# Two pieces ahead, a clamp on another engine, squares on ScalarE and transposes in one step, in a kernel of attention and a squared-ReLU feed-forward

## The chip, the cores and the metric

The kernel runs on one core of one Trainium2 chip. The metric is the device time of one execution in microseconds (us). Five engines work side by side, each on its own instructions in the order in which they were issued: PE (matmuls), DVE (vector operations), ACT (activation functions and copies), POOL (vector operations) and SP, which here issues all the large DMAs. An engine that needs another's result waits on a semaphore, and everything behind the waiting instruction on its engine waits too. PE writes to PSUM, which the kernel uses as eight banks of 128 x 512 fp32.

## The reference

```python
def _attn_ref(q, k, v, g_q, g_k):          # q, k, v: (8, 12, 448, 64)
    def rmsnorm(x, g):
        rms = np.sqrt(np.mean(x * x, axis=-1, keepdims=True) + 1e-06)
        return x / rms * g
    q_n, k_n = (rmsnorm(q, g_q), rmsnorm(k, g_k))
    scores = 1.0 / np.sqrt(64) * np.matmul(q_n, k_n.transpose(0, 1, 3, 2))
    scores = scores - np.max(scores, axis=-1, keepdims=True)
    attn = np.exp(scores)
    attn = attn / (np.sum(attn, axis=-1, keepdims=True) + 1e-09)
    return np.matmul(attn, v)
...
x = attn_out.transpose(0, 2, 1, 3).reshape(3584, 768)
h = np.maximum(x @ w_in, 0.0)              # w_in: (768, 2048)
return h * h @ w_out                       # w_out: (2048, 768)
```

The inputs are fp32, but the feed-forward weights come to the kernel as 8-byte floating point words and are converted on the chip.

## The kernel before

The heads are worked on in pairs: 8 batches of 6 pairs, 48 in all. A pair has four steps (`n` or `m` from 0 to 3, 112 keys each). In a step PE computes the scores of both heads (`weigh`, L212), ACT takes the exponentials out of two PSUM banks (L214), and PE multiplies the previous pair's weights with its values (`attend`, L272) and with ones for the sums (L279, or L283 where DVE and POOL have added the weights up first, `add_up`). A reciprocal of the sums (L294) and a product (`finish`, L304) on DVE give the pair's part of x.

Ahead of this a pair is prepared: `load_qk` three pairs ahead, `square` (ACT, L154) at step 1 and `normalize` at step 2 of the pair two before it (sums on DVE, L162 and L163; the power -1/2 on POOL, L167; q times it on POOL into a tile `qn`, L172; the factor of k goes into the exponential). `turn` (L191) transposes q and k on PE into a bank; DVE evicts q with the gain (L193), ACT evicts k (L195). In the first 12 pairs (`alone`) the transposes of q go to bank 2 and those of k to bank 3, at steps 0 and 2 of the pair before; scores use banks 0 and 1 in even steps and 2 and 3 in odd ones. Later pairs use bank 2 for both transposes.

The feed-forward takes two batches as a unit, and unit u runs beside the attention of unit u + 1, as a generator that is advanced in proportion to the steps; the last unit runs alone at the end. So the span has four stages: attention alone (first 12 pairs), then attention with units 0, 1 and 2 of the feed-forward, then unit 3. A unit has 4 blocks. A block is two rounds of first products and one round of second products, each in Strassen's manner with seven products (names P1 to P7) in place of eight. Costs are counted in units: 18 for a first product, 126 for a round, 502 for a block, 2008 for a unit. `hidden` finishes a part of the middle values: DVE adds (L422), ACT takes the Relu (L423), POOL squares (L424). The second products begin with the 64 left-over rows of each batch (L451) and go on with L468; DVE and ACT add up the results (L499, L501).

The weights are converted in 64 pieces of 128 x 384, four to a tile. `load_weights` brings 8-byte words into a tile `words`; `split_words` scales the high words on ACT (L568), clamps them on POOL (L569) and turns the low words into numbers on ACT (L573, L574); `join_words` builds fp32 on DVE (L583, L587, L591). After a tile's fourth piece, four sums of pieces are made, DVE and POOL in turn (`make_sums`, L617), and the tile is stored to DRAM for the later units (L619). One call of `convert` makes sums, joins the piece that is begun, loads the next and splits its own. Calls have due times: 16 pieces every 2.4 steps in stage 1 (`early`), and 48 beside unit 0 (`late`), at every 18 cost units in bursts, one at each block. The order of all of this on all engines is the order of the program, since the scheduling is by hand.

`program` is built twice, with and without a shift of the scores; the inputs take the one without.

Of the kernel before, what the change touches and what calls it, by code (L numbers as in the profile page):

```python
# [10 lines left out]
F32 = mybir.dt.float32  # L11
# [7 lines left out]
P = 128  # L19
# [55 lines left out]
def program(ctx, tc, q, k, v, g_row, moe_w_in, moe_w_out, out, shift):  # L75
# [50 lines left out]
    def load_qk(i):  # L126
        b, c = pairs[i]
        qk = io.tile([CP, 2, 2 * NJ, D], F32, name="qk", tag="qk")
        nc.sync.dma_start(
            qk[:, 0].rearrange("p (h j) d -> p h (j d)", j=NJ),  # L130
            q[b, 2 * c : 2 * c + 2].rearrange("h (p j) d -> p h (j d)", j=NJ),
        )
        for e in range(2):
            nc.sync.dma_start(
                qk[:, 1].rearrange("p (j h) d -> p j h d", h=2)[:, :, e],
                k[b, 2 * c + e].rearrange("(p j) d -> p j d", j=NJ),
            )
        loaded[i] = qk
# [18 lines left out]
    def normalize(i):  # L157

        qk = loaded.pop(i)
        ms = small.tile([CP, 4 * NJ], F32, name="ms", tag="ms", bufs=2)  # L160
        for x, squares in enumerate(squared.pop(i)):
            nc.vector.tensor_reduce(out=ms[:, ts(x, 2 * NJ)], in_=squares, axis=AX.X, op=ALU.add)  # L162
        nc.vector.tensor_scalar(  # L163
            out=ms, in0=ms, scalar1=1.0 / D, scalar2=1e-6, op0=ALU.mult, op1=ALU.add
        )
        rr = small.tile([CP, 2, 2 * NJ], F32, name="rr", tag="rr", bufs=4)
        nc.gpsimd.tensor_tensor(  # L167
            out=rr.rearrange("p x r -> p (x r)"), in0=ms,
            in1=minus_half.to_broadcast([CP, 4 * NJ]), op=ALU.pow,
        )  # L170
        qn = att.tile([CP, NJ, 2, D], F32, name="qn", tag="qn", bufs=1)
        nc.gpsimd.tensor_tensor(  # L172
            out=qn.rearrange("p j h d -> p h j d"),
            in0=qk[:, 0].rearrange("p (h j) d -> p h j d", j=NJ),
            in1=rr[:, 0].rearrange("p (h j) -> p h j", j=NJ)[:, :, :, None].to_broadcast([CP, 2, NJ, D]),
            op=ALU.mult,
        )
        kn = qk[:, 1]
        if shift:
            nc.gpsimd.tensor_tensor(  # L180
                out=kn, in0=kn, in1=rr[:, 1, :, None].to_broadcast([CP, 2 * NJ, D]), op=ALU.mult
            )
        normal[i] = qn, kn.rearrange("p (j h) d -> p j h d", h=2), rr[:, 1]

    def turn(i, x):

        rows = normal[i][x]
        tr = banks[2 + x if alone(i) else 2][:, 0:S]
        dst = att.tile([P, S], F32, name="qT" if x == 0 else "kT")
        for j in range(NJ):  # L190
            nc.tensor.transpose(tr[:, ts(j, CP)], rows[:, j].rearrange("p h d -> p (h d)"), ident[:CP, :CP])  # L191
        if x == 0:
            nc.vector.tensor_scalar(out=dst, in0=tr, scalar1=g, scalar2=None, op0=ALU.mult)  # L193
        else:
            nc.scalar.copy(dst, tr)  # L195
        turned[i, x] = dst
# [5 lines left out]
    def weigh(i, m):  # L202

        if shift:
            return weigh_shifted(i, m)
        new_weights(i, m)
        qT, kT = turned[i, 0], turned[i, 1]
        odd = (2, 3) if alone(i) else (4, 6) if between(i) else (0, 1)
        scs = [banks[odd[e] if m % 2 else e][:CP, 0:S] for e in range(2)]
        for e, sc in enumerate(scs):  # L210
            r = ds(e * D, D)
            nc.tensor.matmul(sc, lhsT=kT[r, ts(m, CP)], rhs=qT[r, :], start=True, stop=True)  # L212
        for e, sc in enumerate(scs):
            nc.scalar.activation(  # L214
                weights[i, e, m], sc, AF.Exp, scale=normal[i][2][:, 2 * m + e : 2 * m + e + 1]
            )
        add_up(i, m)
# [14 lines left out]
    def weigh_shifted(i, m):  # L232
# [5 lines left out]
        for e in range(2):  # L238
# [4 lines left out]
            nc.vector.tensor_reduce(out=nmax, in_=sc, axis=AX.X, op=ALU.max, negate=True)  # L243
            w = att.tile([CP, S], F32, name="w", tag="rden", bufs=1)
            nc.scalar.activation(w, sc, AF.Exp, bias=nmax)
# [17 lines left out]
    def attend(i, m):  # L263
# [22 lines left out]
        if m == (NJ - 1 if alone(i) else 1):  # L286
            rden = att.tile([P, S], F32, name="rden", tag="rden", bufs=1)
            if shift:
                nc.vector.tensor_scalar(
                    out=rden, in0=den, scalar1=1e-9, scalar2=None, op0=ALU.add  # L290
                )
                nc.vector.reciprocal(out=rden, in_=rden)
            else:
                nc.vector.reciprocal(out=rden, in_=den)  # L294
            dens[i] = rden
# [4 lines left out]
    def finish(i):  # L300

        b, c = pairs[i]
        xT = new_x()
        nc.vector.tensor_tensor(out=xT, in0=values_bank(i), in1=dens.pop(i), op=ALU.mult)  # L304
        xts[b, c] = xT
# [115 lines left out]
    def hidden(dst, ps, part, op):  # L421
        nc.vector.tensor_tensor(out=dst, in0=ps, in1=part, op=op)  # L422
        nc.scalar.activation(dst, dst, AF.Relu)  # L423
        nc.gpsimd.tensor_tensor(out=dst, in0=dst, in1=dst, op=ALU.mult)  # L424

# [106 lines left out]
    all_pieces = list(weight_pieces())  # L532
    words, targets, sums_to_make = {}, {}, deque()

# [7 lines left out]
    def load_weights(n):  # L542
        if n >= len(all_pieces) or moe_w_in.dtype == F32:
            return
        kind, t, form, rows = all_pieces[n]
        words[n] = ffn_p.tile([P, HALF, 2], U32, name="words", tag="words")
        rows = rows.bitcast(U32)
# [16 lines left out]
    def split_words(n):  # L564
        if n not in words:
            return
        low, high = words[n][:, :, 0], words[n][:, :, 1]
        nc.scalar.activation(high.bitcast(F32), high.bitcast(F32), AF.Copy, scale=REBIAS)  # L568
        nc.gpsimd.tensor_scalar(  # L569
            out=high.bitcast(F32), in0=high.bitcast(F32), scalar1=MOST, scalar2=-MOST,  # L570
            op0=ALU.min, op1=ALU.max,
        )
        nc.scalar.activation(low.bitcast(F32), low, AF.Copy, scale=2.0**-29, bias=2.0**23)  # L573
        nc.scalar.activation(low, low.bitcast(F32), AF.Copy, bias=-(2.0**23))  # L574

    def join_words(n):
        kind, t, form, rows = all_pieces[n]
        dst = target(n)
        if n in words:
            both = words.pop(n)  # L580
            low, high = both[:, :, 0], both[:, :, 1]
            bits = dst.bitcast(U32)
            nc.vector.tensor_scalar(  # L583
                out=bits, in0=high, scalar1=4, scalar2=1,
# [16 lines left out]
    def make_weight_forms(kind, dst, t):  # L601
# [8 lines left out]
        sums_to_make.extend(todo)  # L610
        sums_to_make.append(((in_forms if kind == "in" else out_forms)[t], dst))

    def make_sums():

        for engine in (nc.vector, nc.gpsimd) if sums_to_make else ():
            to, left, right, op = sums_to_make.popleft()
            engine.tensor_tensor(out=to, in0=left, in1=right, op=op)  # L617
        if sums_to_make and len(sums_to_make[0]) == 2:
            nc.sync.dma_start(*sums_to_make.popleft())  # L619
# [42 lines left out]
    with tc.manual_schedule(engines=ENGINES):  # L662
# [8 lines left out]
        for i, (b, c) in enumerate(pairs):  # L671
            u = b // 2
            for n in range(NJ):
# [71 lines left out]
```

## Time and profile before

| | |
|---|---|
| median of three runs | 1703.6 us (1702.66 to 1704.24) |
| the profiled execution's own time | 1708.85 us |
| its span, first to last instruction | 1707.0 us |
| mean granted PE clock in it | 0.966 |
| loads of q, one for a pair | 48 of 224 KB |
| loads of k, two for a pair | 96 of 112 KB |
| loads of weight words | 64 of 384 KB |

Times in the profile are of one execution. A row of its timeline has the start in us, the length, the engine, the line of the kernel, what is written and read, and the count; in brackets stands how long the engine was idle before and what ended that. A row of the waits has the engine and line, what was waited for, the sum in us, the number and the longest. Matmuls overlap in PE's pipeline, so the length of a row is not its pace; the distance between starts is.

### The profile page before, as it was taken

The numbers are of one execution on the slowest core, as the hardware profiler recorded it, in microseconds if no ns is written. First come the engines' busy times: TensorE is split into PE (matmuls) and PEld (weight loads), VectorE is DVE, ScalarE is ACT, GpSimd is POOL, SyncE is SP. The second block draws the span as 40 slices with busy tenths as digits, with TensorE's granted clock in tenths as the row PEclk, the third lists the DMA queues.
The fourth block names the chain that finished last, engine by engine and source line by source line (L and its number), as shares of the span: only waits on it lengthen the run. The fifth ranks groups of instructions, "written<-read, shape, count | busy, mean of one in ns | idle before, by whom it ended". The sixth has DMA issues, their size and how long they took to land.

```text
span 1707.0 us, 14931 instructions
## 1 busy us (share of the span) xinstructions
PE 1573.1 (92%) x5204; PEld 719.2 (42%) x5204; DVE 808.6 (47%) x1170; ACT 554.3 (32%) x1033; POOL 614.1 (36%) x490
## 2 busy tenths in 40 slices
PE   5888897978969989999998999999998999999997
PEld 2222243433434434444444444444444444555554
DVE  2654546476676556343534445343535444213323
ACT  4554443452441423333131223333132221220120
POOL 4333545253353453424323354424223332210211
PEclk9999998988989989999999999999999999999999
DMA  3443213253242334303131324203131313132112
GB/s 97 121 127 113 86 46 125 63 164 118 63 159 100 125 116 145 100 25 133 54 123 49 111 77 162 90 19 137 49 122 49 128 38 139 65 125 88 65 74 67
DMA packets 98777, 164.65 MB, mean 96 GB/s; under 512 B 49028, under 2 KB 82820, under 8 KB 90500
## 3 DMA queue, kind: packets, MB, share of 16 engines
q1 hardware_dynamic: 98688, 163.60, 28.8%
q8 instruction: 43, 0.70, 0.2%
q14 instruction: 42, 0.34, 0.1%
q10 hardware_dynamic: 4, 0.00, 0.0%
HBM read 128.98 MB, written 34.60 MB: 96 GB/s over the span
## 4 chain that ended last, share of the span: by engine, by line
PE 72%; DVE 7%; issue 6%; POOL 6%; DMA 5%; ACT 3%; SPq 0%; POOLq 0%; ACTq 0%; DVEq 0%
PE bank L468 24%; PE bank L402 23%; PE bank L212 9%; PE bank L272 8%; PE bank L451 3%; DMA words<-in_moe_w_in_dram 3%; DMA words<-in_moe_w_out_dram 3%; PE bank L191 2%; DVE rden L294 2%; POOL rr L167 2%; POOL hid L424 2%; PE bank L279 1%; PE bank L283 1%; ACT wT L214 1%; ACT words L568 1%
## 5 line engine op out<-in xcount | busy, mean ns | idle before, releaser
L402 PE MATMUL bank<-xT,in_sb 128*128 128x448 f32 x1344 | 526.8, 546 | 2.5 <-DVE xT L304 2.5
L214 ACT ACTIVATE wT<-bank,rr 112x448 f32<-112x448 f32 x384 | 222.7, 628 | 438.8 <-PE bank L212 434.9
L402 PEld LDWEIGHTS bank<-xT,in_sb 128*128 128x128 f32 x1344 | 251.3, 192 | 255.5 <-issue 241.1
L468 PE MATMUL bank<-out_sb,hid 128*128 128x384 f32 x768 | 274.7, 487 | 2.1 <-DVE acc L501 2.1
L212 PE MATMUL bank<-qT,kT 64*112 64x448 f32 x768 | 220.3, 613 | 60.4 <-ACT wT L214 38.7
L167 POOL TENSOR_TENSOR rr<-ms,minus_half 112x16 f32<-112x16 f32 x48 | 150.7, 3140 | 339.6 <-DVE ms L163 329.6
L424 POOL TENSOR_TENSOR hid<-hid 128x448 f32<-128x448 f32 x128 | 123.1, 972 | 406.3 <-ACT hid L423 406.3
L501 DVE TENSOR_TENSOR acc<-acc,bank 128x384 f32<-128x384 f32 x324 | 173.4, 550 | 198.8 <-PE bank L468 161.1
L294 DVE RECIPROCAL rden<-bank 128x448 f32<-128x448 f32 x48 | 141.9, 2957 | 154.0 <-PE bank L283 99.6
L468 PE MATMUL bank<-out_sb,sums 128*128 128x384 f32 x576 | 214.3, 495 | 0.0
L272 PE MATMUL bank<-wT,vt 112*64 112x448 f32 x768 | 195.9, 591 | 3.6 <-DVE xT L304 3.6
L468 PEld LDWEIGHTS bank<-out_sb,hid 128*128 128x128 f32 x768 | 144.6, 190 | 105.7 <-issue 4.9
L422 DVE TENSOR_TENSOR hid<-bank,part 128x448 f32<-128x448 f32 x128 | 76.2, 615 | 177.9 <-PE bank L402 177.3
L409 ACT COPY part<-bank 128x448 f32<-128x448 f32 x128 | 67.7, 531 | 263.1 <-PE bank L402 263.1
L468 PEld LDWEIGHTS bank<-out_sb,sums 128*128 128x128 f32 x576 | 106.8, 192 | 83.5 <-issue 15.6
L212 PEld LDWEIGHTS bank<-qT,kT 64*112 64x112 f32 x768 | 62.8, 179 | 176.9 <-issue 77.0
L451 PE MATMUL bank<-out_sb,hid 128*128 128x384 f32 x256 | 100.7, 537 | 34.9 <-POOL hid L424 34.9
L423 ACT ACTIVATE hid<-hid 128x448 f32<-128x448 f32 x128 | 72.0, 576 | 179.1 <-DVE hid L422 179.1
L230 DVE TENSOR_TENSOR sum<-sum,wT 112x448 f32<-112x448 f32 x72 | 65.1, 904 | 122.8 <-ACT wT L214 120.1
L230 POOL TENSOR_TENSOR sum<-sum,wT 112x448 f32<-112x448 f32 x72 | 85.1, 1182 | 55.4 <-ACT wT L214 52.3
L272 PEld LDWEIGHTS bank<-wT,vt 112*64 112x64 f32 x768 | 39.6, 139 | 139.2 <-issue 122.6
L569 POOL TENSOR_SCALAR words<-words 128x384 f32<-128x384 f32 x64 | 40.9, 640 | 156.7 <-ACT words L568 156.7
(55 smaller groups left out, 1070.7 us busy)
## 6 DMA issues: line engine op xcount, KB each, us to landing
out_sb<-out_forms SPq DMA_DIRECT2D x24, 1536.0 KB, 7.5
in_sb<-in_forms SPq DMA_DIRECT2D x24, 1344.0 KB, 5.7
words<-in_moe_w_in_dram SPq DMA_DIRECT2D x32, 384.0 KB, 3.3
words<-in_moe_w_out_dram SPq DMA_DIRECT2D x32, 384.0 KB, 3.4
out_forms<-out_sb SPq DMA_DIRECT2D x8, 1536.0 KB, 6.1
qk<-in_q_dram SPq DMA_DIRECT2D x48, 224.0 KB, 2.7
qk<-in_k_dram SPq DMA_DIRECT2D x96, 112.0 KB, 2.9
vt<-in_v_dram SPq DMA_DIRECT2D x48, 224.0 KB, 2.8
```

The costliest lines, as they stand in the source:

```text
L167: nc.gpsimd.tensor_tensor(out=rr.rearrange("p x r -> p (x r)"), in0=ms, in1=minus_half.to_broadcast([CP, 4 * NJ]), op=ALU.pow,)
L212: nc.tensor.matmul(sc, lhsT=kT[r, ts(m, CP)], rhs=qT[r, :], start=True, stop=True)
L214: nc.scalar.activation(weights[i, e, m], sc, AF.Exp, scale=normal[i][2][:, 2 * m + e : 2 * m + e + 1])
L230: engine.tensor_tensor(out=sums[i, e], in0=sums[i, e], in1=weights[i, e, m], op=ALU.add)
L272: nc.tensor.matmul(av[ds(e * D, D), :], lhsT=values[i][:, e, m, :], rhs=weights[i, e, m], start=m == 0, stop=m == NJ - 1,)
L294: nc.vector.reciprocal(out=rden, in_=den)
L402: nc.tensor.matmul(ps, lhsT=w_sb[:, IN.index(left), c, :], rhs=forms[u, c][right], start=first and c == 0, stop=c == NK - 1, skip_group_ch ...
L422: nc.vector.tensor_tensor(out=dst, in0=ps, in1=part, op=op)
L424: nc.gpsimd.tensor_tensor(out=dst, in0=dst, in1=dst, op=ALU.mult)
L451: nc.tensor.matmul(ps, lhsT=flat[a][:, t, ds(FULL, P)], rhs=w_sb[t][:, 2 * a + half, :], start=a == 1 and t == 0, stop=a == 0 and t == 1,)
L468: nc.tensor.matmul(ps, lhsT=lefts[left][:, t, ts(tt, P)], rhs=w_sb[t][:, OUT.index(right), :], start=first and t == 0, stop=t == 1, skip_g ...
L501: nc.vector.tensor_tensor(out=acc, in0=acc, in1=ps, op=ALU.add)
```

## The change

- `load_qk` loads q as it loads k: one transfer for a head, the two heads side by side in rows. `normalize` multiplies q in place; the tile `qn` is gone.
- `turn` runs for x = 0 and 1 both at step 1 where the current pair is among the first 12, with banks 2 and 3; otherwise at steps 0 and 2 as before.
- The reciprocal is written into a buffer of the pool of x, and `finish` multiplies in place; the tile `rden` is gone.
- `hidden` squares on ACT.
- `words` has three buffers; pieces are loaded two ahead (a second load stands before the loop).
- The clamp moves from `split_words` on POOL to `join_words` on DVE.
- Stores of finished tiles have a queue of their own and are issued at the start of the first `convert` that finds no sums left; each list of conversions has one more slot at its end.

```diff
     def load_qk(i):
...
-        nc.sync.dma_start(
-            qk[:, 0].rearrange("p (h j) d -> p h (j d)", j=NJ),
-            q[b, 2 * c : 2 * c + 2].rearrange("h (p j) d -> p h (j d)", j=NJ),
-        )
-        for e in range(2):
-            nc.sync.dma_start(
-                qk[:, 1].rearrange("p (j h) d -> p j h d", h=2)[:, :, e],
-                k[b, 2 * c + e].rearrange("(p j) d -> p j d", j=NJ),
-            )
+        for x, rows in enumerate((q, k)):
+            for e in range(2):
+                nc.sync.dma_start(
+                    qk[:, x].rearrange("p (j h) d -> p j h d", h=2)[:, :, e],
+                    rows[b, 2 * c + e].rearrange("(p j) d -> p j d", j=NJ),
+                )
...
-        qn = att.tile([CP, NJ, 2, D], F32, name="qn", tag="qn", bufs=1)
-        nc.gpsimd.tensor_tensor(
-            out=qn.rearrange("p j h d -> p h j d"),
...
+        for x in range(2 if shift else 1):
             nc.gpsimd.tensor_tensor(
...
+                out=qk[:, x], in0=qk[:, x], in1=rr[:, x, :, None].to_broadcast([CP, 2 * NJ, D]),
+                op=ALU.mult,
             )
...
-        tr = banks[2 + x if alone(i) else 2][:, 0:S]
+        tr = banks[2 + x if alone(max(i - 1, 0)) else 2][:, 0:S]
...
-            rden = att.tile([P, S], F32, name="rden", tag="rden", bufs=1)
+            rden = new_x()
...
-        xT = new_x()
-        nc.vector.tensor_tensor(out=xT, in0=values_bank(i), in1=dens.pop(i), op=ALU.mult)
+        xT = dens.pop(i)
+        nc.vector.tensor_tensor(out=xT, in0=values_bank(i), in1=xT, op=ALU.mult)
...
         nc.scalar.activation(dst, dst, AF.Relu)
-        nc.gpsimd.tensor_tensor(out=dst, in0=dst, in1=dst, op=ALU.mult)
+        nc.scalar.activation(dst, dst, AF.Square)
...
-        words[n] = ffn_p.tile([P, HALF, 2], U32, name="words", tag="words")
+        words[n] = ffn_p.tile([P, HALF, 2], U32, name="words", tag="words", bufs=3)
...
         nc.scalar.activation(high.bitcast(F32), high.bitcast(F32), AF.Copy, scale=REBIAS)
-        nc.gpsimd.tensor_scalar(
-            out=high.bitcast(F32), in0=high.bitcast(F32), scalar1=MOST, scalar2=-MOST,
-            op0=ALU.min, op1=ALU.max,
-        )
...
             bits = dst.bitcast(U32)
+            nc.vector.tensor_scalar(
+                out=high.bitcast(F32), in0=high.bitcast(F32), scalar1=MOST, scalar2=-MOST,
+                op0=ALU.min, op1=ALU.max,
+            )
...
-        sums_to_make.append(((in_forms if kind == "in" else out_forms)[t], dst))
+        forms_to_store.append(((in_forms if kind == "in" else out_forms)[t], dst))
...
-        if sums_to_make and len(sums_to_make[0]) == 2:
-            nc.sync.dma_start(*sums_to_make.popleft())
...
     def convert(more):
+        for store in (forms_to_store.popleft(),) if len(sums_to_make) == 0 and forms_to_store else ():
+            nc.sync.dma_start(*store)
         make_sums()
...
-            load_weights(n + 1)
+            load_weights(n + 2)
...
-        return [(first + every * n, n < 4 * tiles) for n in range(4 * tiles + 3)]
+        return [(first + every * n, n < 4 * tiles) for n in range(4 * tiles + 4)]
...
     load_qk(1)
+    load_weights(1)
...
-                if n % 2 == 0 and i < last:
-                    turn(i + 1, n // 2)
+                if i < last:
+                    for x in range(2):
+                        if n == (1 if alone(i) else 2 * x):
+                            turn(i + 1, x)
```

More of the change, by code (lines that the diff above doesn't have):

```diff
@@ L170, in normalize @@
         )
-        qn = att.tile([CP, NJ, 2, D], F32, name="qn", tag="qn", bufs=1)
-        nc.gpsimd.tensor_tensor(
-            out=qn.rearrange("p j h d -> p h j d"),
-            in0=qk[:, 0].rearrange("p (h j) d -> p h j d", j=NJ),
-            in1=rr[:, 0].rearrange("p (h j) -> p h j", j=NJ)[:, :, :, None].to_broadcast([CP, 2, NJ, D]),
-            op=ALU.mult,
-        )
-        kn = qk[:, 1]
-        if shift:
+        for x in range(2 if shift else 1):
             nc.gpsimd.tensor_tensor(
-                out=kn, in0=kn, in1=rr[:, 1, :, None].to_broadcast([CP, 2 * NJ, D]), op=ALU.mult
+                out=qk[:, x], in0=qk[:, x], in1=rr[:, x, :, None].to_broadcast([CP, 2 * NJ, D]),
+                op=ALU.mult,
             )
-        normal[i] = qn, kn.rearrange("p (j h) d -> p j h d", h=2), rr[:, 1]
+        normal[i] = [qk[:, x].rearrange("p (j h) d -> p j h d", h=2) for x in range(2)], rr[:, 1]
     def turn(i, x):
-        rows = normal[i][x]
-        tr = banks[2 + x if alone(i) else 2][:, 0:S]
+        rows = normal[i][0][x]
+        tr = banks[2 + x if alone(max(i - 1, 0)) else 2][:, 0:S]
         dst = att.tile([P, S], F32, name="qT" if x == 0 else "kT")
@@ L214, in weigh @@
             nc.scalar.activation(
-                weights[i, e, m], sc, AF.Exp, scale=normal[i][2][:, 2 * m + e : 2 * m + e + 1]
+                weights[i, e, m], sc, AF.Exp, scale=normal[i][1][:, 2 * m + e : 2 * m + e + 1]
             )
@@ L243, in weigh_shifted @@
             nc.vector.tensor_reduce(out=nmax, in_=sc, axis=AX.X, op=ALU.max, negate=True)
-            w = att.tile([CP, S], F32, name="w", tag="rden", bufs=1)
+            w = ffn_p.tile([CP, S], F32, name="w", tag="part", bufs=4)
             nc.scalar.activation(w, sc, AF.Exp, bias=nmax)
@@ L532, in program @@
     all_pieces = list(weight_pieces())
-    words, targets, sums_to_make = {}, {}, deque()
+    words, targets, sums_to_make, forms_to_store = {}, {}, deque(), deque()
     def target(n):
@@ L568, in split_words @@
         nc.scalar.activation(high.bitcast(F32), high.bitcast(F32), AF.Copy, scale=REBIAS)
-        nc.gpsimd.tensor_scalar(
-            out=high.bitcast(F32), in0=high.bitcast(F32), scalar1=MOST, scalar2=-MOST,
-            op0=ALU.min, op1=ALU.max,
-        )
         nc.scalar.activation(low.bitcast(F32), low, AF.Copy, scale=2.0**-29, bias=2.0**23)
```

## The prediction

> **What bounds the kernel now.** I read the page first, then what TensorE (PE) waited for, then equal pieces of work in two stretches of the span, and last the order of time around single stalls.
>
> ```profile
> span 1707.0 us, 14931 instructions
> ...
> PE 1573.1 (92%) x5204; PEld 719.2 (42%) x5204; DVE 808.6 (47%) x1170; ACT 554.3 (32%) x1033; POOL 614.1 (36%) x490
> ...
> PEclk9999998988989989999999999999999999999999
> ...
> PE 72%; DVE 7%; issue 6%; POOL 6%; DMA 5%; ACT 3%; SPq 0%; POOLq 0%; ACTq 0%; DVEq 0%
> ```
>
> PE is the bound, yet 28% of the chain that ended last is not PE, and the granted clock shows an 8 only between the 7th and the 15th of the 40 slices. So the reserve lies in the early stages. The two stretches below go from the same place of the first feed-forward unit to the same place of the second (start of the second products of block 0 to those of block 3):
>
> ```profile
> 262.00:623.00 361.00, 303.61 (x916) 137.63 (x916) 223.78 (x320) 144.10 (x282) 150.77 (x137) 0.90 0.35 116
> 724.00:1005.00 281.00, 275.40 (x918) 127.39 (x919) 121.57 (x168) 83.97 (x154) 95.18 (x70) 0.99 0.24 84
> ```
>
> Columns: stretch, length, busy time and count of PE, weight loads, DVE, ACT, POOL, then clock, DMA share, GB/s. PE runs the same instructions (916 and 918), but the first stretch takes 80 us more. What differs is that weight pieces are converted in it: 152 more DVE instructions, 102 us of DVE. The largest single wait of PE shows how this costs time:
>
> ```profile
> 594.60 0.52 POOL L569 TENSOR_SCALAR words<-words 128x384 f32<-128x384 f32 x1
> 594.65 0.33 SPq L619 DMA_DIRECT2D out_forms<-out_sb  x1
> 595.10 0.36 SPq L554 DMA_DIRECT2D words<-in_moe_w_out_dram  x1
> ...
> 602.10 0.54 ACT L568 ACTIVATE words<-words 128x384 f32<-128x384 f32 x1 [12.44 <-DMA words<-in_moe_w_out_dram]
> ...
> 604.21 2.36 PE L212 MATMUL bank<-qT,kT 64*112 64x448 f32 x4 [9.50 <-ACT wT L214]
> ```
>
> A piece's load is issued only when the piece before the last is joined, here behind a 1.5 MB store. ACT, which works in order, stands 12.44 us before that piece, the exponentials queue behind it, and PE stands 9.50 us before a bank that they should have emptied. Then its four score matmuls take 2.36 us in place of 1.01.
>
> Stage 1 (the first 12 pairs, attention alone) has another limit:
>
> ```profile
> 34.65 1.01 PE L212 MATMUL bank<-qT,kT 64*112 64x448 f32 x4 [0.85 <-DVE qT L193]
> ...
> 48.03 1.01 PE L212 MATMUL bank<-qT,kT 64*112 64x448 f32 x4 [1.18 <-DVE qT L193]
> ...
> 50.62 1.01 PE L212 MATMUL bank<-qT,kT 64*112 64x448 f32 x4
> ...
> 53.22 0.60 PE L191 MATMUL bank<-ident,qk 112*128 112x112 f32 x4
> 53.75 1.69 PE L212 MATMUL bank<-qT,kT 64*112 64x448 f32 x4
> ...
> 61.43 1.01 PE L212 MATMUL bank<-qT,kT 64*112 64x448 f32 x4 [1.21 <-DVE qT L193]
> ...
> 77.42 1.84 PE L212 MATMUL bank<-qT,kT 64*112 64x448 f32 x4 [3.79 <-DVE qT L193]
> ...
> 121.69 1.84 PE L212 MATMUL bank<-qT,kT 64*112 64x448 f32 x4 [2.46 <-DVE qT L193]
> ...
> 187.49 1.01 PE L212 MATMUL bank<-qT,kT 64*112 64x448 f32 x4 [2.40 <-DVE qT L193]
> ```
>
> Each pair stops PE at step 1: the scores need bank 2, which the q transposes of step 0 have just filled and DVE has not yet emptied. At step 3 the same holds for bank 3 (1.69 instead of 1.01). From 34.65 to 187.49 are ten pairs: 15.28 us each. PE alone needs per step 2.60 (50.62 to 53.22) and per transpose group 0.53, so 4 x 2.60 + 2 x 0.53 = 11.46 us.
>
> **The change part by part.**
>
> *Both transposes at step 1 (stage 1).* They now fill banks 2 and 3 after the scores of step 1, and the next user is step 3, one whole step of 2.60 us later. DVE's queue decides whether that is enough:
>
> ```profile
> 62.47 1.16 ACT L214 ACTIVATE wT<-bank,rr 112x448 f32<-112x448 f32 x2 [1.72 <-PE bank L212]
> ...
> 70.55 2.96 DVE L294 RECIPROCAL rden<-bank 128x448 f32<-128x448 f32 x1 [4.88 <-PE bank L279]
> ...
> 76.69 0.67 DVE L193 TENSOR_SCALAR qT<-bank,g 128x448 f32<-128x448 f32 x1
> ```
>
> The reciprocal comes at the end of step 3, conversions may follow it, then the eviction of q. In the bad pair the reciprocal began at 70.55 and q was out at 77.36, 6.81 us later; scores of step 3 would come 2.60 (step 0) + 2.60 + 1.06 + 2.60 = 8.86 us after it. So even the bad pair fits. A new wait is added: the transposes need the exponentials of step 1 out of banks 2 and 3. These end 62.47 + 1.16 - 61.43 = 2.20 us after the scores start, and PE arrives after 2.60: 0.40 us of cover. Behind waiting transposes stands all of PE, behind the waiting ACT copy of k the squares and the next exponentials. Gain per pair: between nothing and 15.28 - 11.46 = 3.82 us. I take 12.2 us per pair, as the slow-clock pairs should go with the gaps but DVE grows: 10 x 3.08 = **31 us**, bounds 0 and 38.
>
> A rule bears on this. The Trainium skill, "TensorE: Matmul & The Clock Gate", Part 1, says that PE falls to half rate after an idle window of about 3.4 us. By it only the 3.79 us gap above should bring slow matmuls; the row at 121.69 shows 1.84 us after a gap of 2.46. So the trace disagrees, and short gaps are worth removing too; by the rule I would expect fewer slow pairs to vanish and some 10 us less.
>
> *Two pieces ahead, three buffers, stores one conversion later.* The load has a whole conversion more: at the pace of the second stretch (281 us for 1506 cost units) an 18-unit conversion is 3.36 us. In the stall above the data came 7.0 us after its issue, which two such intervals nearly cover. The ACT wait, and with it the score waits, should mostly go:
>
> ```profile
> PE bank L212 <- ACT wT L214: 38.7, 10, 9.5
> ```
>
> *Clamp from POOL to DVE, 64 times.* The trace has no such clamp on DVE. Nearest rows, of operations with the same size:
>
> ```profile
> L569 POOL TENSOR_SCALAR words<-words x64: 522/538/1253, 22.0 to 602.7; 128x384 f32<-128x384 f32 x64
> ...
> L583 DVE TENSOR_SCALAR in_sb<-words x32: 343/350/1975, 28.9 to 522.7; 128x384 uint32<-128x384 uint32 x32
> ...
> L587 DVE SCALAR_TENSOR_TENSOR in_sb<-words,in_sb x32: 557/559/2046, 29.3 to 523.1; 128x384 uint32<-128x384 uint32 x32
> ...
> L617 DVE TENSOR_TENSOR in_sb<-in_sb x16: 494/550/3895, 61.3 to 531.7; 128x384 f32<-128x384 f32 x16
> ```
>
> (minimum/median/maximum ns.) Bounds 0.34 and 1.98 us; I take 0.45, nearest L583, which reads the same words with the same kind of instruction. The hand-over ACT to POOL to DVE becomes ACT to DVE, so POOL's queue no longer delays a join. Is DVE full then? Conversions fill 990 of 1506 cost units of the stretch (108 + 342 + 342 + 198 by the lists of due times), 185 us at the second stretch's pace. In it DVE has 0.433 x 185 = 80 us of other work, 102 us of conversions as they ran, and about 43 clamps x 0.45 = 19: 201 us in 185. With all conversions at their short durations (0.35 clamp, 0.35, 0.56, 0.56 and half a sum 0.27, 2.1 us x 43 = 90) it is 170. So between 0 and 16 us over, 30 at a clamp of 0.77. With in-order delays of evictions I leave 25 of the 80 us: **55 us**, bounds 25 and 80.
>
> The port rule would give more. The Trainium skill, "SBUF — State Buffer", section "SBUF: two separate sides", says that DVE and POOL take turns on a shared pair of ports, whole instructions at a time; the row of L617 (550 median, 3895 longest) agrees. By it, less POOL work shortens the joins and stage 2 gives some 75 us; that is the third case below.
>
> *Squares of the middle values from POOL to ACT.* Stage 3 and 4 wait for these only:
>
> ```profile
> PE bank L451 <- POOL hid L424: 12.1, 8, 4.3
> ...
> PE bank L451 <- POOL hid L424: 2.5, 8, 0.4
> ```
> ```profile
> L423 ACT ACTIVATE hid<-hid x128: 561/577/581, 225.6 to 1663.6; 128x448 f32<-128x448 f32 x128
> ...
> L424 POOL TENSOR_TENSOR hid<-hid x128: 927/932/1424, 226.2 to 1664.2; 128x448 f32<-128x448 f32 x128
> ```
> ```profile
> 902.62 3.21 POOL L167 TENSOR_TENSOR rr<-ms,minus_half 112x16 f32<-112x16 f32 x1
> ...
> 909.19 0.93 POOL L424 TENSOR_TENSOR hid<-hid 128x448 f32<-128x448 f32 x1
> ...
> 910.18 6.50 PE L451 MATMUL bank<-out_sb,hid 128*128 128x384 f32 x10 [4.33 <-POOL hid L424]
> ...
> 1470.77 3.49 PE L451 MATMUL bank<-out_sb,hid 128*128 128x384 f32 x10 [0.23 <-POOL hid L424]
> ```
>
> The waits are 12.1 us (stretch 650 to 1436) and 2.5 (from there on). The square stands behind POOL's power and sums (902.62 to 909.19), and after two such waits of 4.33 the ten matmuls take 6.50 instead of 3.49: 6 us more. On ACT a square costs 0.577, as the Relu before it, against 0.932: 128 x 0.577 = 74 us on an engine that is 32% busy, hidden by its idle time; without that cover an exponential comes 0.6 us later. PE gains 14.6 + 6 less some 5 that stays: **15 us**, bounds 6 and 20.
>
> *The rest.* q normalised in place does the same POOL work. q now comes in two transfers in place of one:
>
> ```profile
> qk<-in_q_dram SPq DMA_DIRECT2D x48, 224.0 KB, 2.7
> qk<-in_k_dram SPq DMA_DIRECT2D x96, 112.0 KB, 2.9
> ```
>
> 48 more issues on SP, landing 2.9 instead of 2.7 us, two steps ahead of use: nothing, but about 0.7 us at the very start, where nothing covers it. There the later transposes of pair 1 let a second score step run first, some 1.7 us. Net **1 us** gain. The reciprocal goes into the buffer of x, one step earlier out of 32: nothing, or a DVE wait of a few us at the end of a unit if they run out.
>
> **Sum.** 31 + 55 + 15 + 1 = 102 us off the span of 1707.0: 1605. The runs have a median of 1703.6, 3.4 below that span, so **1602 us**.
>
> **The rivals.**
> 1. *DVE takes the place of the loads as the limit.* Clamps and joins run as long as beside POOL. Stage 2 keeps 50 of its 80 us (25 more than I leave), stage 1 gains 20 in place of 31: 102 - 36 = 66, 1638 us. For it: 201 us of demand in 185. Against it: POOL loses 43 x 0.54 us and the squares there, and DVE was 62% busy in the stretch (223.78 of 361).
> 2. *Everything goes to PE's pace*: 5 us left in stage 2, stage 1 at 11.6 us a pair: 75 + 37 + 16 + 2 = 130, 1574 us. For it: the second stretch, which does that. Against it: it has no conversions.
> 3. *Slower: the clamp is held.* If a clamp on DVE is held by a POOL instruction as one sum was (3.9 us), in order before the evictions for PE, 64 cost 250 us in place of 29: 102 turns to a loss of about 119, 1823 us. It decides from about 102 / 64 = 1.6 us more per clamp. Against it: L583's median of 350 in the same queue.
> 4. *The loads stay late.* If the third buffer only moves the wait (the load still follows a join, and DVE is late with that) and stage 1's transposes wait for exponentials in place of DVE, the 55 and the 31 us are gone, and if clamps beside the evictions cost the 15 of the squares too, 1 us is left: 1703 us. Against it: the load of a piece no longer follows the join right before its own split, but one conversion earlier.
>
> **Chances.** My forecast (1575 to 1635) 0.69, rival 1 0.15, rival 2 0.10, rival 3 0.04, rival 4 0.02. The range takes the forecast with most of rivals 1 and 2: 1568 to 1655. A measurement tells about 0.2% (3.4 us) from no change. Faster: the forecast and rivals 1 and 2, 0.94; same: rival 4, 0.02; slower: rival 3, 0.04.
>
> **What would show it.** Right: ten pairs of stage 1 near 122 us with no wait for qT at step 1; the stretch between the same places of the first unit near 305 us at a clock of 0.95 or more; hardly any ACT wait of L568 for a DMA; waits of L451 under 5 us from unit 2 on; clamps at 0.35 to 0.5 us. Wrong: transposes that wait for wT in stage 1 (then its gain falls), evictions by DVE that end PE's waits in the bursts (rival 1), clamps above 1 us (rival 3).

## The result, and the profile after

The changed kernel takes 1587.5 us (median of four runs, 1586.0 to 1588.1) against 1703.8 before: a ratio of 0.932 with a 95% interval of 0.930 to 0.933. The profiled execution took 1587.84 us, its span is 1586.0. The page of the changed kernel, its head, the clock row and the chain by engine:

```profile
span 1586.0 us, 15000 instructions
...
PE 1523.8 (96%) x5204; PEld 703.3 (44%) x5204; DVE 821.0 (52%) x1234; ACT 622.0 (39%) x1161; POOL 454.3 (29%) x298
...
PEclk9999999999999999999999999999999999999999
...
PE 89%; DVE 5%; ACT 4%; issue 1%; POOL 0%; DMA 0%; POOLq 0%; ACTq 0%; DVEq 0%
```

PE stands for 89% of the chain in place of 72%, and DMA and POOL have left it. The clock row has no 8 any more (the mean granted clock is 0.991 in place of 0.966). Line numbers have moved by some ten: L441 is the first second product (L451 before), L202 the scores (L212), L181 the transposes (L191), L414 the square (L424), L558 the first ACT operation on words (L568).

To see where the time went, the span is divided at two places that both kernels pass: the first run of ten L441 (block 0 of the first unit), and the same of block 3. The timeline of PE in the changed kernel, start and length in us:

```profile
214.00 3.49 PE L441 MATMUL bank<-out_sb,hid 128*128 128x384 f32 x10 [0.78 <-ACT hid L414]
...
312.80 5.03 PE L441 MATMUL bank<-out_sb,hid 128*128 128x384 f32 x10 [4.48 <-ACT hid L414]
...
416.99 5.18 PE L441 MATMUL bank<-out_sb,hid 128*128 128x384 f32 x10 [3.37 <-ACT hid L414]
...
518.91 3.49 PE L441 MATMUL bank<-out_sb,hid 128*128 128x384 f32 x10 [0.40 <-ACT hid L414]
```

The kernel before passes these four places at 261.86, 382.70, 507.40 and 623.23. So 47.9 us were won up to the first place, 361.4 - 304.9 = 56.5 between them, and 1083.8 - 1067.1 = 16.7 after them: 121 us in all. The same two places divide the span of every kernel below:

| kernel | median us | ratio to before [95%] | to block 0 | block 0 to 3 | rest of the span |
|---|---|---|---|---|---|
| before | 1703.8 | | 261.9 | 361.4 | 1083.8 |
| changed | 1587.5 | 0.932 [0.930, 0.933] | 214.0 | 304.9 | 1067.1 |
| e1: transposes alone | 1678.2 | 0.984 [0.982, 0.986] | 234.4 | 358.3 | 1082.4 |
| e9: loads alone | 1655.7 | 0.970 [0.968, 0.973] | 251.5 | 318.1 | 1083.2 |
| e2: transposes undone | 1627.2 | 0.954 [0.952, 0.956] | 256.2 | 302.1 | 1066.2 |
| e3: loads one ahead | 1624.8 | 0.954 [0.951, 0.957] | 219.2 | 334.6 | 1067.7 |
| e4: clamp on POOL | 1587.2 | 0.931 [0.929, 0.932] | 213.4 | 305.3 | 1065.7 |
| e5: squares on POOL | 1618.4 | 0.948 [0.946, 0.950] | 214.1 | 317.7 | 1083.2 |
| e6: two clamps | 1602.1 | 0.938 [0.936, 0.940] | 215.4 | 317.7 | 1067.5 |
| e7: conversions spread | 1575.3 | 0.922 [0.921, 0.924] | 214.5 | 293.0 | 1066.0 |
| e11: stores early | 1592.1 | 0.934 [0.932, 0.936] | 218.7 | 304.0 | 1067.0 |
| e13: spread, clamp on POOL | 1574.4 | 0.924 [0.922, 0.925] | 214.2 | 292.7 | 1066.2 |
| e12: gaps | 1567.0 | 0.920 [0.918, 0.921] | 213.9 | 283.9 | 1067.3 |
| e14: gaps, early table load | 1566.3 | 0.918 [0.915, 0.920] | 212.5 | 284.2 | 1067.8 |

The first part, in the same timeline of the changed kernel:

```profile
31.48 1.01 PE L202 MATMUL bank<-qT,kT 64*112 64x448 f32 x4
...
34.08 0.99 PE L181 MATMUL bank<-ident,qk 112*128 112x112 f32 x8
34.99 1.01 PE L202 MATMUL bank<-qT,kT 64*112 64x448 f32 x4
...
45.37 0.98 PE L181 MATMUL bank<-ident,qk 112*128 112x112 f32 x8
...
56.66 0.98 PE L181 MATMUL bank<-ident,qk 112*128 112x112 f32 x8
...
146.97 0.98 PE L181 MATMUL bank<-ident,qk 112*128 112x112 f32 x8
...
156.87 1.01 PE L202 MATMUL bank<-qT,kT 64*112 64x448 f32 x4 [0.59 <-DVE xT L294]
```

A pair takes 11.29 us, and ten pairs 112.89 (34.08 to 146.97): all ten at the same pace, without a wait, where ten took 152.84 before (the last row shown is already step 1 of the 13th pair, in the next stage). Over these ten pairs the mean granted clock is 1.00 in place of 0.92. The eight transposes of a pair now run as one row of 0.91 us (34.08 to the scores at 34.99), where two groups of 0.53 took 1.06.

The second part, in the changed kernel's waits of ACT between 214 and 519, and the two lines of the kernel before that answer to it (between 262 and 623), then the windows of the changed kernel in that stretch and in the unit after it, with the columns of the prediction:

```profile
ACT words L558 <- DMA words<-in_moe_w_in_dram: 10.7, 6, 2.7
```
```profile
ACT words L568 <- DMA words<-in_moe_w_in_dram: 50.3, 12, 13.9
...
ACT words L568 <- DMA words<-in_moe_w_out_dram: 44.1, 13, 12.4
```
```profile
214.00:519.00 305.00, 281.76 (x917) 128.54 (x917) 232.38 (x366) 157.63 (x307) 100.06 (x69) 0.97 0.41 135
616.00:893.00 277.00, 275.26 (x927) 127.31 (x925) 122.35 (x170) 99.11 (x182) 73.44 (x46) 1.00 0.26 86
```

ACT's waits for loads fell from 94 us to 11, the longest from 13.9 to 2.7. With them went PE's waits for the exponentials. This is what is left of them in the whole span of the changed kernel, 38.7 us before:

```profile
PE bank L202 <- ACT wT L204: 0.4, 1, 0.4
```

Of the 56 us, 34 are idle time of PE (57 us before, 23 after) and 22 are busy time (303.61 and 281.76 us for the same matmuls, at a mean granted clock of 0.90 and 0.97). DVE is now busy for 232 of 305 us, while the next unit, which has no conversions, takes 277 for about the same PE instructions.

### The profile page after: what moved, and what is told of

It is laid out like the page before. It is cut to its first block, busy times and chain, and to the rows that moved or that the text cites. A ratio compares the mean times of both kernels' runs of the same rounds, so it can differ in the third digit from the quotient of the medians.

```text
span 1586.0 us, 15000 instructions
## 1 busy us (share of the span) xinstructions
PE 1523.8 (96%) x5204; PEld 703.3 (44%) x5204; DVE 821.0 (52%) x1234; ACT 622.0 (39%) x1161; POOL 454.3 (29%) x298
## 4 chain that ended last, share of the span: by engine, by line
PE 89%; DVE 5%; ACT 4%; issue 1%; POOL 0%; DMA 0%; POOLq 0%; ACTq 0%; DVEq 0%
PE bank L392 29%; PE bank L458 28%; PE bank L202 11%; PE bank L262 10%; PE bank L441 4%; PE bank L181 3%; PE bank L269 2%; PE bank L273 2%; DVE xT L284 1%; ACT hid L414 1%; ACT hid L413 1%; DVE sum L220 1%; ACT wT L204 1%; DVE hid L412 1%; DVE in_sb L607 0%
## 5 line engine op out<-in xcount | busy, mean ns | idle before, releaser
L458 PE MATMUL bank<-out_sb,hid 128*128 128x384 f32 x768 | 277.0, 490 | 9.0 <-DVE acc L491 9.0
L284 DVE RECIPROCAL xT<-bank 128x448 f32<-128x448 f32 x48 | 141.9, 2957 | 117.3 <-PE bank L273 99.2
L202 PE MATMUL bank<-qT,kT 64*112 64x448 f32 x768 | 199.8, 595 | 1.6 <-ACT kT L185 0.6
L262 PE MATMUL bank<-wT,vt 112*64 112x448 f32 x768 | 188.3, 570 | 2.9 <-DVE xT L294 2.9
L458 PEld LDWEIGHTS bank<-out_sb,sums 128*128 128x128 f32 x576 | 105.6, 190 | 81.9 <-issue 13.4
L435 POOL TENSOR_TENSOR sums<-hid,sums 128x768 f32<-128x768 f32 x16 | 29.3, 1829 | 298.6 <-PE bank L441 182.1
L441 PE MATMUL bank<-out_sb,hid 128*128 128x384 f32 x256 | 93.2, 508 | 16.0 <-ACT hid L414 16.0
L202 PEld LDWEIGHTS bank<-qT,kT 64*112 64x112 f32 x768 | 55.6, 175 | 114.4 <-issue 58.8
L183 DVE TENSOR_SCALAR qT<-bank,g 128x448 f32<-128x448 f32 x48 | 32.7, 682 | 95.8 <-PE bank L181 95.8
```

The costliest lines, as they stand in the source:

```text
L262: nc.tensor.matmul(av[ds(e * D, D), :], lhsT=values[i][:, e, m, :], rhs=weights[i, e, m], start=m == 0, stop=m == NJ - 1,)
L441: nc.tensor.matmul(ps, lhsT=flat[a][:, t, ds(FULL, P)], rhs=w_sb[t][:, 2 * a + half, :], start=a == 1 and t == 0, stop=a == 0 and t == 1,)
L458: nc.tensor.matmul(ps, lhsT=lefts[left][:, t, ts(tt, P)], rhs=w_sb[t][:, OUT.index(right), :], start=first and t == 0, stop=t == 1, skip_g ...
```

## The experiments

**e1, the transposes alone.** The kernel before with this edit only:

```diff
-        tr = banks[2 + x if alone(i) else 2][:, 0:S]
+        tr = banks[2 + x if alone(max(i - 1, 0)) else 2][:, 0:S]
...
-                if n % 2 == 0 and i < last:
-                    turn(i + 1, n // 2)
+                if i < last:
+                    for x in range(2):
+                        if n == (1 if alone(i) else 2 * x):
+                            turn(i + 1, x)
```

> The kernel before with the one edit that both transposes run at step 1 of the first 12 pairs. Theory (the eviction of q out of bank 2 is stage 1's limit, and the slow PE clock there follows from its gaps): stage 1 falls from 15.3 to about 11.5-12 us a pair, 1703.6 falls by 30 to 40 us to about 1668, with no PE wait for qT in stage 1, and nothing changes in the later stages. Rival (DVE's queue, with conversions that wait for POOL's clamp, and late loads hold stage 1 too): under 20 us, about 1688, with new waits of the transposes for exponentials.

27.5 us were won ahead of block 0 and 4.5 after it; no PE wait for qT is left. This is less than the theory had, and the wait that the rival named is there. From the timeline of e1:

```profile
127.67 0.34 SPq L619 DMA_DIRECT2D out_forms<-out_sb  x1
128.18 0.33 SPq L554 DMA_DIRECT2D words<-in_moe_w_out_dram  x1
...
135.79 0.54 ACT L568 ACTIVATE words<-words 128x384 f32<-128x384 f32 x1 [8.97 <-DMA words<-in_moe_w_out_dram]
...
138.00 0.98 PE L191 MATMUL bank<-ident,qn 112*128 112x112 f32 x4 [8.18 <-ACT wT L214]
```

A load behind a store holds ACT for 8.97 us, ACT's exponentials hold banks 2 and 3, and the transposes wait 8.18 us. So the transposes' new wait is real, but only where a load is late.

**e2, the transposes undone** in the changed kernel (the edit of e1 the other way round).

> The changed kernel with the transposes back at steps 0 and 2. Theory: stage 1 goes back to its chain of reciprocal, product and eviction, 13.4 us a pair at least: 1587.5 plus 22 to 40, about 1618. Rival (loads, clamp and stores had made up stage 1): under 10 us more.

Measured 40 us more; ahead of block 0 it is 42.2 (256.2 against 214.0), and the stretch behind it takes 2.8 less. The chain is back, with early loads and the clamp on DVE all the same: 13.4 us for the shortest pairs, and 148.07 for ten (36.48 to 184.55):

```profile
36.48 1.01 PE L202 MATMUL bank<-qT,kT 64*112 64x448 f32 x4 [0.85 <-DVE qT L183]
...
49.86 1.01 PE L202 MATMUL bank<-qT,kT 64*112 64x448 f32 x4 [1.19 <-DVE qT L183]
...
63.26 1.01 PE L202 MATMUL bank<-qT,kT 64*112 64x448 f32 x4 [1.21 <-DVE qT L183]
...
184.55 1.01 PE L202 MATMUL bank<-qT,kT 64*112 64x448 f32 x4 [2.41 <-DVE qT L183]
```

**e3, one piece ahead** in the changed kernel:

```diff
-    load_weights(1)
...
-        words[n] = ffn_p.tile([P, HALF, 2], U32, name="words", tag="words", bufs=3)
+        words[n] = ffn_p.tile([P, HALF, 2], U32, name="words", tag="words")
...
-            load_weights(n + 2)
+            load_weights(n + 1)
```

> The changed kernel with weight pieces loaded one ahead into two buffers again. Theory (ACT's wait for a load, with the exponentials behind it, was the main loss beside the first unit): most of the 56 us that the stretch of the first unit gained are lost, about 30 to 45 us more, some 1625, with ACT waits of L558 for the DMA of over 50 us in that stretch. Rival (POOL's queue with clamp and squares was the loss, and the loads only showed it): under 10 us more, about 1595.

Measured 37 us more: 29.7 between block 0 and block 3 and 5.2 ahead of it. The waits of ACT in e3 between 219 and 554:

```profile
ACT words L558 <- DMA words<-in_moe_w_in_dram: 40.5, 11, 7.3
...
ACT words L558 <- DMA words<-in_moe_w_out_dram: 21.7, 10, 5.8
```

62 us of waits in place of 11. The theory holds, but not alone: with late loads the stretch still takes 27 us less than before the change (334.6 against 361.4). Of these 27 us the squares account for 12.8 (e5). Of the rest, e3 still has the later stores and the clamp on DVE, and no run separates the two there.

**e9, the loads alone.** The changed kernel with transposes (e1's edit), clamp (e4's) and squares (e5's) as before; left are the loads, the later stores and the buffers that make room.

> Of the change only the loads two ahead in three buffers, with the later stores, q in place and the reciprocal in the pool of x, which make room for it; the transposes, the clamp and the squares are as before. Theory (late loads are the main loss beside the first unit, by themselves): the stretch of 361 us falls by 25 to 35, stage 1 stays at its chain with fewer long pairs: about 1703.6 less 35 to 45, 1663. Rival (POOL's queue delays joins so that the loads stay late without the clamp's and squares' move): less than 15 us gain.

About 50 us were won (0.970): 43.3 in the stretch, 10.4 ahead of it, under 1 in the rest. The rival falls. The 43.3 belong to the early loads and the later stores together. Ahead of block 0 the chain stays, with its long pairs where a conversion stands in DVE's queue between the reciprocal and the eviction of q:

```profile
78.99 1.01 PE L202 MATMUL bank<-qT,kT 64*112 64x448 f32 x4 [3.79 <-DVE qT L183]
```

e1 and e9 together win 27.5 + 10.4 = 38 us ahead of block 0, the whole change 47.9. The 10 us between have no run of their own; they fit what each loses without the other: late loads turn into waits of the transposes (e1), and early loads cannot shorten the chain through bank 2 (e9).

**e4, the clamp on POOL again** in the changed kernel:

```diff
         nc.scalar.activation(high.bitcast(F32), high.bitcast(F32), AF.Copy, scale=REBIAS)
+        nc.gpsimd.tensor_scalar(
+            out=high.bitcast(F32), in0=high.bitcast(F32), scalar1=MOST, scalar2=-MOST,
+            op0=ALU.min, op1=ALU.max,
+        )
...
-            nc.vector.tensor_scalar(
-                out=high.bitcast(F32), in0=high.bitcast(F32), scalar1=MOST, scalar2=-MOST,
-                op0=ALU.min, op1=ALU.max,
-            )
```

> The changed kernel with the clamp on POOL again, between the ACT operations. Theory (POOL's queue delays joins, and through them loads, but two pieces ahead cover most of it; DVE is freed of 64 clamps): 0 to 15 us more, about 1595. Rival 1 (the clamp off POOL was the main gain): 25 us more or above. Rival 2 (DVE is so full beside the first unit that the clamp costs there): 5 to 10 us less, about 1580.

No difference, beyond 1.4 us in any of the three parts. With loads two ahead, the move of the clamp is worth nothing.

**e6, two clamps.** The changed kernel with the DVE instruction of the clamp written twice.

> The changed kernel with the clamp twice in a row on DVE (the second changes nothing in the values): 64 more DVE instructions of 0.35 to 0.5 us. Theory (DVE is the limit inside the bursts beside the first unit): 43 of them lie there, 10 to 17 us more, and nothing in stage 1: about 1600. Rival (DVE has slack there too, as the clamp's removal saved nothing): under 4 us more.

14.5 us more by the medians, 10 by the ratios, and the trace puts 12.8 into the stretch (317.7 against 304.9) and 1.4 ahead of it: 12.8 / 43 = 0.30 us for each clamp in the stretch. So DVE is the limit in the bursts, and a clamp there costs nearly its own 0.35 us. As e4 shows no gain without it, POOL's clamp should cost as much by its own way. This is argued, and the waits fit it: in e4 DVE is busy for 14 us less in the stretch than in the changed kernel, but its joins wait 25 us for POOL's clamp. The clamp in the changed kernel, minimum, median and maximum in ns:

```profile
L569 DVE TENSOR_SCALAR words<-words x64: 296/354/1979, 28.2 to 505.3; 128x384 f32<-128x384 f32 x64
```

**e5, the squares on POOL again** in the changed kernel:

```diff
-        nc.scalar.activation(dst, dst, AF.Square)
+        nc.gpsimd.tensor_tensor(out=dst, in0=dst, in1=dst, op=ALU.mult)
```

> The changed kernel with the squares of the middle values on POOL again. Theory (the square on POOL stood behind the power and the sums there and held the first second products of every block): the waits of L441 go from 16 back to about 35 us, with 6 us of slow clock behind the long ones: 20 to 30 us more, about 1612; the stretch of the first unit, 305 us now, takes 10 to 15 more. Rival (with the clamp gone POOL is quick enough): under 8 us more.

31 us more by the medians, 27 by the ratios: 12.8 in the stretch and 16.1 in the rest. PE's wait for the squares in e5; below it the same wait in the changed kernel, and PE's wait for accumulations there, which is 3.3 us in e5:

```profile
PE bank L441 <- POOL hid L414: 36.6, 22, 9.5
```
```profile
PE bank L441 <- ACT hid L414: 16.0, 14, 4.5
...
PE bank L458 <- DVE acc L491: 9.0, 2, 6.3
```

**e11, stores early** in the changed kernel: in `convert`, `make_sums()` stands ahead of the store in place of behind it.

> The changed kernel with each finished tile's store issued right behind the last sums, as before the change, and not one conversion later. Theory (a store in front of a load cost time only because the load was needed at once; two pieces ahead the load has over 3 us more): within 4 us of 1587.5. Rival (the order of store and load was a part of the gain, since SP waits for POOL's sum before the store and the load stands behind it): 8 us more or above, with ACT waits of L558 for the DMA of over 30 us.

4.5 us more by the medians, 4 by the ratios, at the edge of the theory's bound. All of it lies ahead of block 0 (218.7 against 214.0), and ACT's waits for words stay small (9.7 us). What the early store holds up is another load. The timeline of e11:

```profile
130.95 0.63 ACT L151 ACTIVATE squares<-qk 112x512 f32<-112x512 f32 x1 [4.90 <-DMA qk<-in_q_dram]
...
133.03 1.53 PE L202 MATMUL bank<-qT,kT 64*112 64x448 f32 x4 [2.35 <-ACT wT L204]
```

The loads of q and k come behind a store that was issued at 122.48, ACT waits 4.90 us with the exponentials behind it, and PE 2.35, about half of the difference.

**e7, conversions spread.** In the changed kernel, the step of both lists of `late` is 22 in place of `COST_IN` (18).

> The changed kernel with the conversions beside the first unit every 22 cost units in place of every 18, so that the same work is spread over more of each block. Theory (what is left there, 305 us against 277 to 281 in the unit after it, is DVE's backlog in the bursts, through its late evictions and late middle values): 8 to 15 us less, about 1577. Rival (what is left comes from single collisions of DVE and POOL sums on shared ports at the start of the second products, whatever the spacing): within 3 us of 1587.5.

11.9 us less in the stretch and 12 in the time (16 by the ratios): the density of the bursts was half of what is left. That it costs time through DVE rests on e6, since e7 spreads the work of ACT, POOL and the loads as well. In e7 the waits at blocks 1 and 2 remain:

```profile
310.78 6.49 PE L441 MATMUL bank<-out_sb,hid 128*128 128x384 f32 x10 [4.47 <-ACT hid L414]
...
409.09 5.13 PE L441 MATMUL bank<-out_sb,hid 128*128 128x384 f32 x10 [3.70 <-ACT hid L414]
```

**e13, spread with the clamp on POOL** (e7 and e4 together).

> Every 22 cost units, and the clamp on POOL again. Theory (a clamp beside the first unit costs DVE 0.30 us, as the doubled clamp showed, and POOL's clamp as much through its queue and the joins that it holds): within 3 us of the 1575.3 with the clamp on DVE. Rival (once the bursts are spread, POOL's slack is free and DVE's is not): 5 us less or better, 1570.

The same time as e7; the rival falls.

**e12, gaps ahead of the second products.** The changed kernel with due times that leave out the last three first products of a block. They leave out the start of the second products too: in blocks 1 and 2 none lies between 201 and 293 of a block's 502 units, and second products begin at 252.

```diff
-    late = deque(conversions(2, product + 2 * COST_IN, COST_IN))
-    for blk in range(1, NBLK):
-        late.extend(conversions(4 if blk < NBLK - 1 else 2, blk * block + 1, COST_IN))
+    second = 2 * product
+    late = deque((162 + 18 * n if n < 2 else second + 22 + 20 * (n - 2), n < 8) for n in range(12))
+    for blk in range(1, NBLK - 1):
+        late.extend(
+            (blk * block + (1 + 20 * n if n < 11 else second + 41 + 22 * (n - 11)), n < 16)
+            for n in range(20)
+        )
+    late.extend(((NBLK - 1) * block + 1 + COST_IN * n, n < 8) for n in range(12))
```

> The changed kernel with other due times beside the first unit: conversions every 18 to 22 cost units, but none during the last three first products ahead of a block's second products, so that DVE and ACT are free for the last middle values there. Theory (the two waits of L441 of 3.4 to 4.5 us, and the slow clock behind them, come from conversions in DVE's queue in front of the last sums): these waits fall under 1.5 us and the stretch from 293 (every 22) to about 285: 1567. Rival (the backlog only moves, to the accumulations at the start of the second products): 1572 to 1580, with PE waits for acc.

1567.0 us, a ratio of 0.920 [0.918, 0.921], 20 us below the changed kernel.

```profile
307.33 4.94 PE L441 MATMUL bank<-out_sb,hid 128*128 128x384 f32 x10 [2.67 <-ACT hid L414]
...
405.57 3.49 PE L441 MATMUL bank<-out_sb,hid 128*128 128x384 f32 x10 [1.75 <-ACT hid L414]
...
497.80 3.49 PE L441 MATMUL bank<-out_sb,hid 128*128 128x384 f32 x10 [0.40 <-ACT hid L414]
```

The stretch takes 283.9 us, where about 285 was expected. From block 1 to block 3 it takes 190.5 us, e7 196.7 and the changed kernel 206.1. The waits halved, to 2.67 and 1.75; they did not fall under 1.5 as expected. As the edit changes the spacing and keeps the start of the second products free as well, the run does not tell which of these gave the 9 us over e7.

**e14, the table load early.** e12 with one square of a single element on ACT behind the two memsets ahead of the loop.

> The kernel with the gaps in the conversions, and one square of a single element on ACT ahead of the first squares, so that the activation table is loaded while q is on its way. Theory (the second transfer of q gave the first square two things to wait for, and the table load now stands behind the first of them, 1.28 us on the way to the first transposes): the first transposes start at about 14.0 in place of 15.3 us, and the time falls by 1 to 1.5 us from 1567.0, at the edge of what can be measured. Rival (the first transposes wait for k's or q's landing anyway): they start at 15.0 or later, no difference.

1566.3 us, a ratio of 0.918 [0.915, 0.920], which can't be told from e12. The timeline of its start:

```profile
3.82 1.28 ACT L649 ACT_TABLE_LOAD   x1 [3.82 <-DVE bounded L64]
...
8.81 0.63 ACT L151 ACTIVATE squares<-qk 112x512 f32<-112x512 f32 x1 [0.61 <-DMA qk<-in_k_dram]
...
14.54 1.75 PE L181 MATMUL bank<-ident,qk 112*128 112x112 f32 x8 [9.94 <-POOL qk L169]
```

The load of the table is out of the way and the first transposes start at 14.54 in place of 15.33; then the landing of k holds them, so that 0.8 of the expected 1.3 us came.

## Why the prediction was right, step by step

The forecast was 1602 us in a range from 1568 to 1655; 1587.5 lies in it, 121 us of span were won where 102 were forecast. By its terms:

- **Transposes at step 1**, 31 us for ten pairs: measured 152.84 - 112.89 = 40.0. The bank wait, the cover of 0.40 us for the exponentials and the end of the slow pairs were read right; the term that was mis-sized is the 12.2 us a pair, which measured 11.29. The pace reached PE's own, and passed the 11.46 that was meant as the floor, as eight transposes in a row cost 0.91 and not 1.06. Without this part (e2) ten pairs take 148.07, so 35 of the 40 us hang on it; e1 shows that it needs early loads for the last of them.
- **Loads, clamp and stores beside the first unit**, 55 us: measured 56.5. The main cause is right (e9: 43; e3: 30 lost without the early load). That the size fits is in part luck, since the parts that the term names gave 43.7 (e5: 361.4 - 317.7) and another part made up the rest: the clamp's move, which the prediction counted as a relief for the joins, is worth nothing with loads two ahead (e4), and the squares, which it counted only for the later stages, are worth 12.8 us here (e5).
- **DVE's price of the clamp**, 0.45 us within 0.34 to 1.98: median 0.354. DVE as the limit in the bursts was right: e6 adds 0.30 us for each clamp, and e7 takes 12 us away by spreading alone. The 25 us left of the 80 came out as 304.9 - 281 = 24, but only because the squares helped here: with them on POOL it is 37 (e5). Rival 1 asked for more than DVE's backlog cost.
- **Squares on ACT** in the later stages, 15 us: 16.7 measured, 16.1 lost again in e5.
- **The rest**, 1 us. The start gained 3.2 (the scores of step 1 of the second pair begin at 31.48 in place of 34.65): 5.0 by the transposes (36.48 in e2, without them) less 1.8. The 0.7 us for the first transfers was mis-sized: the first transposes came 1.8 us later. The timelines of the kernel before and of the changed one:

```profile
3.81 1.28 ACT L154 ACT_TABLE_LOAD   x1 [3.81 <-DVE bounded L64]
...
13.54 1.01 PE L191 MATMUL bank<-ident,qn 112*128 112x112 f32 x4 [8.95 <-POOL qn L172]
```
```profile
7.71 1.28 ACT L151 ACT_TABLE_LOAD   x1 [7.71 <-DMA qk<-in_q_dram]
...
15.33 1.01 PE L181 MATMUL bank<-ident,qk 112*128 112x112 f32 x4 [10.73 <-POOL qk L169]
```

- From step 1 of the 13th pair, the first behind stage 1, to block 0 (200.29 to 261.86 before, 156.87 to 214.00 after) 4.4 us were won for which the prediction had no term. PE's waits for squares there fell from 4.3 us to 0.8, but with the squares on POOL again (e5: 155.81 to 214.13) only 1.2 are lost. Where the rest comes from stays open.

The difference to the forecast is then 40 + 3 - 32 = 11 us in stage 1, 4 in that last piece, and 3 in the two others.

The Trainium skill, "TensorE: Matmul & The Clock Gate", Part 1, has half rate after an idle window of some 3.4 us. The prediction said that shorter gaps count too, and the clock in the kernel before bears it out, though not for every gap: after the gaps of 2.46 us the mean granted clock is 0.50 (121.69 to 127) and 0.70 (171.29 to 177), after the one of 2.40 us it is 1.00 (187.49 to 193), and after those of about 1.2 us it stays at 1.00. What decides between 0.50 and 1.00 after gaps of one length no run shows. With the gaps gone the clock of the ten pairs went from 0.92 to 1.00, and the lower gain that the rule suggested did not come.

## What to carry to other kernels

Where an in-order engine converts what a DMA brings, its wait for a late load is paid by everything behind it, here the exponentials and through them PE; one more buffer and a load issued one step earlier, with the stores moved behind it, were worth 43 us beside the first unit without any other part of the change, and taking the buffer and the early load away again cost 30 there. An eviction that the next step needs at once should get a whole step of slack, by the choice of the step in which its bank is filled; in the ten pairs that was worth 35 us of the 40, with no instruction saved. Once loads are early, look at when the background work is due: the same conversions, spread and kept away from the last results that the next products wait for, gave another 20 us, 12 of them by spreading alone.

## What the runs showed of the hardware

A sum on DVE can be held far longer than one POOL instruction. The changed kernel's timeline:

```profile
421.52 1.73 POOL L607 TENSOR_TENSOR in_sb<-in_sb 128x384 f32<-128x384 f32 x1
...
422.76 4.45 DVE L607 TENSOR_TENSOR in_sb<-in_sb 128x384 f32<-128x384 f32 x1
...
423.20 1.83 POOL L435 TENSOR_TENSOR sums<-hid,sums 128x768 f32<-128x768 f32 x1
...
424.99 1.81 POOL L435 TENSOR_TENSOR hid<-hid 128x768 f32<-128x768 f32 x1
...
433.11 1.65 PE L458 MATMUL bank<-out_sb,hid 128*128 128x384 f32 x2 [6.33 <-DVE acc L491]
```

The sum, 0.55 us by its median, began while POOL was on a sum of its own and ended only after two more POOL instructions in a row. Behind it in DVE's queue stood the joins of two pieces (427.13 to 432.51) and then an accumulation for which PE waited 6.33 us; so the held sum is a part of that wait, not all of it.

The Trainium skill, "SBUF — State Buffer", section "SBUF: two separate sides", has one shared pair of ports held for a whole instruction. The rows agree with that, and add that POOL's next instruction can come before the waiting DVE one.

With two transfers to wait for, the first square put the load of the activation table (1.28 us) behind the first transfer, where with one transfer it ran beside it (rows of the two starts above); e14 takes it out again with one small activation ahead.
